# Splitting the last V load into four pieces and the wo load into twelve, in a decode kernel bound by DMA

## The chip, the cores and the metric

The kernel runs on one core of one Trainium2 chip. The metric is the device time of one execution, in microseconds (us); lower is better. The kernel before repeats within about 0.3 us on most runs, so differences of 1 us can be told, but only from several runs or from the places in the trace where they arise. "Span" is the time from the first to the last instruction in the profile; for differences under 1 us I compare spans and moments in the trace.

The profile calls the engines PE (TensorE, which multiplies matrices), DVE (VectorE), ACT (ScalarE), POOL (GpSimd) and SP (SyncE, which issues the loads; SPq in the lines below); L388 is line 388 of the kernel. It also records which share of TensorE's clock was granted: 1 ("full clock") or 0.5 ("half clock"). Lines of the profile stand here word for word; lines of a view that do not bear on the argument are left out.

## The reference, cut to what matters

Two blocks read the same two tokens (batch 2, one position, 1024 features) and are mixed by a gate: `out = g * attention(x) + (1 - g) * mlp(x)`.

```python
q = (x @ wq) as 32 heads of 128
scores = einsum(q, k_cache) * 128 ** -0.5        # k_cache: 2 x 32 x 16384 x 128, bf16
p = softmax(scores)
o = einsum(p, v_cache)                           # v_cache: the same size
a = o.reshape(2, 1, 4096) @ wo                   # wo: 4096 x 1024
...                                              # the MLP block: w1, w2, w3, w4
return g * a + (1 - g) * b
```

The two caches are 537 of the 572 MB that are read. Each byte is used once, so the kernel can hardly be faster than its loads.

## The kernel before

The caches are worked off in 32 tiles of 8 MB (two heads of one batch row). For each tile K is loaded, transposed on DVE, multiplied with q on PE (S), put through a softmax, and then V is loaded and multiplied (O). Three 8 MB buffers go round in a ring; a load is issued when its buffer is free. wo comes last, in the buffer of the last K, and takes six transfers:

```python
def load_v(i):
    t = big_tile("Vn")                             # 128 x 32768 bf16, 64 KB in a partition
    nc.sync.dma_start(out=t[:].rearrange("p (j d) -> p j d", d=Dh), in_=cache_rows(A_v_cache, i))
    vn_tiles[i] = t

WO_SPLIT = [16, 8, 4, 2, 1, 1]                     # of 32 rows; a row is 2 KB in each partition

def load_wo():
    t = big_tile("wo")[:].rearrange("p (r n) -> p r n", n=D)
    src = A_wo.rearrange("(p r) n -> p r n", p=P)
    r0 = 0
    for n in WO_SPLIT:
        nc.sync.dma_start(out=t[:, r0 : r0 + n, :], in_=src[:, r0 : r0 + n, :])
        r0 += n
```

The work that waits for these loads. Products with a piece of a tile wait only for the transfer that brings this piece.

```python
def pv_rows(V, PT, oc):                            # 64 products, in the order of j
    O = ops.tile([P, 4 * Dh], FP32, name="O")
    for m in range(NM):                            # 16
        for g in range(4):
            j0 = m * CJ + 4 * g
            nc.tensor.matmul(O[32 * g : 32 * g + 32, :], lhsT=PT[:, m : CJ * 32 : 16],
                             rhs=V[:, j0 : j0 + 4, :], start=(m == 0), stop=(m == NM - 1))
    nc.scalar.copy(out=Os[...], in_=O[:])          # then four small float32 products into oc

def wo_stage():                                    # after the last tile
    # ... Q1 = transposes of OT; q_ps = perm product; Q = copy of q_ps: needs every head
    wo = wt.pop("wo").rearrange("k r (p c) -> k r p c", c=KC)
    for r in range(32):
        for c in range(KC):                        # 8
            nc.tensor.matmul(wo_acc[:, c, :], lhsT=wo[:, r, :, c], rhs=Q[:, :, r],
                             start=(r == 0 and c == 0), stop=(r == 31 and c == KC - 1))

# the end: fin = wo_acc * g;  out_pm = fin + pre;  store out_pm (4 KB)
```

Of the kernel before, what the change touches and what calls it, by code (L numbers as in the profile page):

```python
# [23 lines left out]
def kernel(  # L24
# [15 lines left out]
    nc = tc.nc  # L40
    P = nc.NUM_PARTITIONS
    B, Sq, D = A_x.shape
    _, H, Sk, Dh = A_k_cache.shape
# [3 lines left out]
    NJ = G * Sk // P  # L47
# [8 lines left out]
    NT = B * NHG  # L56
# [16 lines left out]
    def big_tile(name):  # L73
        return big.tile([P, SLOT], BF16, tag="big", name=name)
# [7 lines left out]
    kn_tiles = {}  # L82
    vn_tiles = {}
    wt = {}

    def cache_rows(cache, i):
        b, hg = tiles[i]
        return cache[b, hg * G : (hg + 1) * G].rearrange("a s d -> (a s) d").rearrange(
            "(p j) d -> p j d", p=P
        )  # L90
# [7 lines left out]

    def load_v(i):
        t = big_tile("Vn")  # L100
        nc.sync.dma_start(
            out=t[:].rearrange("p (j d) -> p j d", d=Dh), in_=cache_rows(A_v_cache, i)
        )
        vn_tiles[i] = t

    def load_rows(keys, srcs):
# [8 lines left out]
            c0 += R * N  # L115


    WO_SPLIT = [16, 8, 4, 2, 1, 1]

    def load_wo():  # L120
        t = big_tile("wo")[:].rearrange("p (r n) -> p r n", n=D)
# [4 lines that stand above are left out]
# [7 lines left out]
    def load_first():  # L133
# [12 lines left out]
        out=perm[:].rearrange("k (h a) -> k h a", a=4),  # L146
        in_=ident_f[:].rearrange("k (a h) -> k h a", a=4),
# [24 lines left out]
    for g in range(1, 4):  # L172
        nc.vector.tensor_tensor(
            out=osel_f, in0=osel_f, in1=ident_f[:, 40 * g : 40 * g + 8], op=ALU.add
# [4 lines left out]
    for v in range(4):  # L179
        nc.gpsimd.affine_select(  # L180
            out=selv[:, v],
            in_=selv[:, v],
# [306 lines left out]
    for i in range(-1, NT):  # L489
        if i + 1 < NT:  # L490
            xfers.append(("big", f"k{i + 1}", lambda i=i: load_k(i + 1)))
            steps.append((f"k{i + 1}", lambda i=i: (build_z(i + 1), qk_stage(i + 1))))
        if i >= 0:
            xfers.append(("big", f"v{i}", lambda i=i: load_v(i)))
            steps.append((f"v{i}", lambda i=i: pv_stage(i)))
        if i + 1 < NT:
            steps.append(("", lambda i=i: softmax_stage(i + 1)))
        if i in extra:
            xfers.append(("big", f"x{i}", extra[i][0]))
            steps.append((f"x{i}", extra[i][1]))  # L500
# [19 lines left out]
    for name, run in steps:  # L520
# [9 lines left out]
        out=out_pm[:].rearrange("p b r -> p r b"), in0=fin[:], in1=pre[:], op=ALU.add  # L530
# [33 lines left out]
```

## Time and profile before

| | before |
|---|---|
| time, median of 3 runs (lowest to highest) | 1345.77 us (1345.56 to 1345.8) |
| span of the profiled run | 1344.0 us |
| DMA, mean over the span | 427 GB/s |
| last V landed whole | 1315.6 us |
| Q ready | 1324.6 us |
| first wo product, last wo product | 1325.4, 1341.0 us |
| last wo piece landed | 1335.3 us |

The page of the kernel before has the span in 40 slices; a digit is the busy share of the 16 DMA engines in tenths, and below it are the GB/s that they moved.

```profile
DMA  9999999999999999999999999999999999999995
GB/s 406 434 435 432 435 437 423 433 434 432 432 432 440 426 435 432 424 433 435 435 436 428 436 435 434 423 433 438 436 426 433 432 432 433 432 432 435 435 430 220
```

DMA is full until the last slice. A change that leaves the bytes and the instructions alone can save hardly anything outside that slice. The chain of waits that ended last, kernel before, its end (start in us, length in us, what):

```profile
1296.20 29.18 DMA wo<-in_A_wo_dram
1325.39 0.05 issue
1325.43 15.55 PE wo_acc L388 x256
1341.00 0.19 DVE fin L527
1341.21 0.23 DVE out_pm L529
```

The chain runs through the first wo piece and then through 256 wo products without a break. The timeline of the same stretch shows what came before them (start, length, engine, line, operation; in brackets how long the engine had been idle and what it waited for):

```profile
1315.68 6.23 PE L344 MATMUL O<-Vn,PT 128*32 128x512 bf16 x64 [8.89 <-DMA Vn<-in_A_v_cache_dram]
1322.60 1.05 PE L354 MATMUL misc<-osel,Os 128*128 128x2 f32 x8 [0.70 <-ACT Os L352]
1324.38 0.23 DVE L384 CAST Q<-misc 128x64 bf16<-128x64 f32 x1 [0.28 <-PE misc L382]
1325.43 15.53 PE L388 MATMUL wo_acc<-Q,wo 128*128 128x2 bf16 x256 [1.09 <-DMA wo<-in_A_wo_dram]
1341.47 0.40 SPq L533 DMA_DIRECT2D out_dram<-out_pm  x1
```

PE waits 8.9 us for the whole V, takes 6.2 us for its products, needs another 2.7 us until Q is there (1321.91 to 1324.61), waits for the first wo piece and then works off wo at 60 ns a product. The DMA issues of the end (count, KB, us from issue to landing):

```profile
wo<-in_A_wo_dram SPq DMA_DIRECT2D x1, 4096.0 KB, 29.2
wo<-in_A_wo_dram SPq DMA_DIRECT2D x1, 2048.0 KB, 33.7
wo<-in_A_wo_dram SPq DMA_DIRECT2D x2, 256.0 KB, 36.8
out_dram<-out_pm SPq DMA_DIRECT2D x1, 4.0 KB, 1.6
```

The last piece was issued at 1298.5 and landed at 1335.3. PE is busy for 5.7 us after that: products that could have run earlier, had it had work earlier.

One more view is needed. The trace has the semaphore increments of each transfer, one for each of the 16 DMA engines. They show that the engines do not finish together: the last V is done at 1304.7 us on the first engine and at 1315.6 on the last. All "landed" times in this document are those of the last engine.

### The profile page before, as it was taken

How to read it: one execution, taken by the hardware profiler on the slowest of the kernel's cores; microseconds unless marked ns; L12 is line 12 of the kernel's file. 1: busy time of each engine (PE TensorE's matmuls, PEld its weight loads, DVE VectorE, ACT ScalarE, POOL GpSimd, SP SyncE). 2: the span in 40 equal slices, each digit the busy share in tenths (PEclk: the TensorE clock that was granted, in tenths of full speed). 3: DMA queues.
4: the chain of work that ended last, by engine and by line, in shares of the span. 5: the costliest groups of instructions: out<-in, count | busy, mean ns of one | idle time of the engine just before them, and what ended most of it. 6: DMA issues, size and time to landing. Idle time of an engine off the chain costs nothing.

```text
span 1344.0 us, 12921 instructions
## 1 busy us (share of the span) xinstructions
PE 828.4 (62%) x5524; PEld 400.5 (30%) x5587; DVE 707.8 (53%) x864; ACT 45.6 (3%) x100; POOL 14.4 (1%) x45
## 2 busy tenths in 40 slices
PE   2577655576656765555676566655556765555566
PEld 2233222432225322222232423222222322222235
DVE  0666565366651665555565156565445656545560
ACT  0000000000000000000000000000000000000000
POOL 0000000000000000000000000000000000000000
PEclk9988877788776877777887588877778887777885
DMA  9999999999999999999999999999999999999995
GB/s 406 434 435 432 435 437 423 433 434 432 432 432 440 426 435 432 424 433 435 435 436 428 436 435 434 423 433 438 436 426 433 432 432 433 432 432 435 435 430 220
DMA packets 11545, 573.36 MB, mean 427 GB/s; under 512 B 1888, under 2 KB 1888, under 8 KB 2272
## 3 DMA queue, kind: packets, MB, share of 16 engines
q1 hardware_dynamic: 11488, 572.54, 98.7%
q8 instruction: 43, 0.70, 0.2%
q14 instruction: 14, 0.11, 0.0%
HBM read 572.53 MB, written 0.00 MB: 426 GB/s over the span
## 4 chain that ended last, share of the span: by engine, by line
PE 28%; DVE 23%; DMA 19%; another core or an unknown queue 13%; issue 13%; ACT 2%; SPq 0%; ACTq 0%; POOL 0%
DVE T L292 20%; DMA Kn<-in_A_k_cache_dram 17%; PE S L300 13%; PE O L344 7%; PE misc L440 3%; DMA wo<-in_A_wo_dram 2%; PE misc L354 2%; PE misc L207 2%; ACT Pr L328 1%; DVE PT L332 1%; PE wo_acc L388 1%; ACT Os L352 1%; DVE mx L321 1%; DVE mdiag L314 1%
## 5 line engine op out<-in xcount | busy, mean ns | idle before, releaser
L300 PE MATMUL S<-T,z 128*128 128x512 bf16 x1985 | 582.3, 421 | 340.9 <-DVE T L292 319.6
L292 DVE STREAM_TRANSPOSE T<-Kn 128x1024 f32<-128x1024 f32 x512 | 612.0, 1229 | 266.6 <-DMA Kn<-in_A_k_cache_dram 217.6
L300 PEld LDWEIGHTS <-z 128*128 128x128 bf16 x2048 | 218.5, 107 | 699.1 <-issue 537.1
L344 PE MATMUL O<-Vn,PT 128*32 128x512 bf16 x2048 | 120.4, 388 | 8.9 <-DMA Vn<-in_A_v_cache_dram 8.9
L371 DVE TENSOR_TENSOR OT<-misc,rinv 128x2 bf16<-128x2 f32 x32 | 5.1, 159 | 161.4 <-PE misc L354 161.4
L344 PEld LDWEIGHTS <-PT 128*32 128x32 bf16 x2048 | 73.4, 141 | 55.2 <-issue 16.8
L207 PE MATMUL misc<-rs,ones_f 128*128 128x2 f32 x64 | 17.9, 349 | 76.4 <-DVE rs L364 76.4
L352 ACT COPY Os<-O 128x512 f32<-128x512 f32 x32 | 18.8, 586 | 1091.2 <-PE O L344 1091.2
L354 PE MATMUL misc<-osel,Os 128*128 128x2 f32 x256 | 33.7, 254 | 22.2 <-ACT Os L352 22.2
L354 PEld LDWEIGHTS misc<-osel,Os 128*128 128x128 f32 x256 | 31.0, 191 | 36.7 <-ACT Os L352 36.7
L311 DVE TENSOR_REDUCE m<-S 128x1 f32<-128x512 f32 x32 | 22.2, 693 | 36.9 <-PE S L300 36.9
L440 PEld LDWEIGHTS <-wt 128*128 128x128 bf16 x576 | 35.7, 171 | 18.7 <-DMA wt<-in_B_w_dram 17.4
L207 PEld LDWEIGHTS misc<-rs,ones_f 128*128 128x128 f32 x64 | 16.1, 313 | 81.2 <-issue 78.4
L332 DVE STREAM_TRANSPOSE PT<-Pr 128x512 bf16<-128x512 bf16 x32 | 22.7, 711 | 28.7 <-ACT Pr L328 28.7
L328 ACT ACTIVATE Pr<-S,nb 128x512 bf16<-128x512 f32 x32 | 22.0, 687 | 123.6 <-DVE nb L323 120.6
L207 PE MATMUL misc<-mdiag,ones_f 128*128 128x128 f32 x64 | 15.6, 325 | 15.6 <-DVE mdiag L314 15.6
L321 DVE TENSOR_REDUCE mx<-misc 64x1 f32<-64x64 f32 x64 | 14.2, 222 | 19.0 <-PE misc L207 18.6
L270 POOL TENSOR_TENSOR z<-qsel,own 128x32 bf16<-128x32 bf16 x32 | 10.8, 337 | 1225.7 <-PE S L300 1194.5
L245 PE MATMUL misc<-xT,wt 128*128 128x2 bf16 x256 | 7.1, 165 | 25.8 <-DVE xT L240 23.1
L440 PE MATMUL misc<-xn2T,wt 128*128 128x2 bf16 x224 | 14.4, 202 | 9.1 <-DMA wt<-in_B_w_dram 9.1
L440 PE MATMUL misc<-h2T,wt 128*128 128x2 bf16 x224 | 13.6, 198 | 7.9 <-DMA wt<-in_B_w_dram 7.9
L368 DVE RECIPROCAL rinv<-misc 128x2 f32<-128x2 f32 x32 | 5.5, 171 | 22.2 <-PE misc L207 22.2
(74 smaller groups left out, 105.6 us busy)
## 6 DMA issues: line engine op xcount, KB each, us to landing
wt<-in_B_w_dram SPq DMA_DIRECT2D x2, 7168.0 KB, 50.4
wt<-in_B_w_dram SPq DMA_DIRECT2D x2, 2048.0 KB, 39.9
wo<-in_A_wo_dram SPq DMA_DIRECT2D x1, 4096.0 KB, 29.2
wo<-in_A_wo_dram SPq DMA_DIRECT2D x1, 2048.0 KB, 33.7
wo<-in_A_wo_dram SPq DMA_DIRECT2D x1, 1024.0 KB, 35.7
Kn<-in_A_k_cache_dram SPq DMA_DIRECT2D x32, 52.1
Vn<-in_A_v_cache_dram SPq DMA_DIRECT2D x32, 37.8
wo<-in_A_wo_dram SPq DMA_DIRECT2D x1, 512.0 KB, 36.5
```

Of the source, the lines that this page charges most:

```text
L207: nc.tensor.matmul(ps[:], lhsT=ones_f[:], rhs=src, start=True, stop=True)
L292: nc.vector.transpose(out=T[:].rearrange("p w j s -> p j w s"), in_=Kw[:, m * CW : (m + 1) * CW].rearrange("p (j w e) -> p j w e", w=2, e=32),
L300: nc.tensor.matmul(S[:], lhsT=z[:, v, NM - 1 - m : NM - 1 - m + P], rhs=Tb[:, v // 2, :, v % 2], start=(m == 0 and v == 0), stop=(m == NM ...
L311: nc.vector.reduce_max(out=m[:], in_=S[:], axis=AX.X)
L314: nc.vector.tensor_scalar(out=mdiag[:], in0=ident_f[:], scalar1=m[:, 0:1], scalar2=None, op0=ALU.mult)
L321: nc.vector.reduce_max(out=mx[pa, :], in_=mall[pa, pa], axis=AX.X)
L328: nc.scalar.activation(out=Pr[:], in_=S[:], func=ACTF.Exp, bias=nb[:], scale=scale, accum_out=rs[:])
L332: nc.vector.transpose(out=PT[:], in_=Pr[:])
L344: nc.tensor.matmul(O[32 * g : 32 * g + 32, :], lhsT=PT[:, m : CJ * 32 : 16], rhs=V[:, j0 : j0 + 4, :], start=(m == 0), stop=(m == NM - 1),)
L352: nc.scalar.copy(out=Os[:].rearrange("p x d -> p (x d)"), in_=O[:])
L354: nc.tensor.matmul(oc[:], lhsT=Os[:, x, :], rhs=osel[:, x, :], start=(x == 0), stop=(x == 3))
L440: nc.tensor.matmul(ps[:, c, :], lhsT=w[:, r, :].rearrange("k (p c) -> k p c", c=C)[:, :, c], rhs=actT[:, r, :], start=(r == 0), stop=(r == ...
```

## The change

It wants the products to follow the transfers closely. The V products start after half of V, not after all of it, so that only an eighth of them is left when the last byte lands; and the wo products start after 4 of 32 rows, not after 16.

```diff
+    V_SPLIT_LAST = [NJ // 2, NJ // 4, NJ // 8, NJ // 8]
@@ load_v
-        nc.sync.dma_start(
-            out=t[:].rearrange("p (j d) -> p j d", d=Dh), in_=cache_rows(A_v_cache, i)
-        )
+        tv = t[:].rearrange("p (j d) -> p j d", d=Dh)
+        src = cache_rows(A_v_cache, i)
+        j0 = 0
+        for n in V_SPLIT_LAST if i == NT - 1 else [NJ]:
+            nc.sync.dma_start(out=tv[:, j0 : j0 + n, :], in_=src[:, j0 : j0 + n, :])
+            j0 += n
@@
-    WO_SPLIT = [16, 8, 4, 2, 1, 1]
+    WO_SPLIT = [4] * 6 + [2, 2, 1, 1, 1, 1]
```

NJ is 256, the number of V rows of 128 values that each partition holds of a tile; NT is the 32 tiles.

## The prediction

> **What bounds the kernel.** DMA: the page shows the 16 engines 0.9 or more busy in 39 of 40 slices. Nothing before the last slice changes, so only the end counts. There the timeline and the transfers' semaphore increments in the trace show:
> - The last K is used up at 1296.2 us, which issues wo (six pieces) behind the last V.
> - The last V lands whole at 1315.6; its 64 products wait 8.9 us for it, start at 1315.68 and take 6.2 us.
> - Their tail (copy Os, small products, OT, transposes, permutation, Q) runs from 1321.9 to 1324.6, 2.7 us.
> - The first wo piece (16 of 32 rows) lands at 1325.4. Then 256 products run 60.7 ns apart (0.486 us a row), 15.55 us to 1340.98. The last wo piece landed at 1335.3: for the last 5.7 us PE works off a backlog. The chain of waits agrees.
>
> The 16 DMA engines finish a transfer apart (last V: 1304.7 for the first, 1315.6 for the last). A piece counts as landed when the slowest has written; the Trainium skill ("DMA: Bandwidth & Descriptors", section "Why a DMA increments its semaphore by 16 and not by 1") says the same, and this trace agrees. That engine takes 0.61 us a wo row, longer than PE's 0.486, so PE can keep up if it starts in time.
>
> **What the change does.** V in 1/2, 1/4, 1/8, 1/8 should land at about 1305.7, 1310.8, 1313.3, 1315.9. 56 of 64 products then hide under the transfer; the last eight take about 0.9 us at the half clock seen here, so Q is ready at about 1319.6 instead of 1324.6. wo in pieces of four rows lands every 2.5 us from about 1318.4, so PE starts at 1319.6 instead of 1325.4, catches up by the third or fourth piece and then waits for each. The end is the last landing plus one row's products.
>
> **What it adds.** Smaller packets: by median record 2 KB takes 84 ns, 4 KB 160, 8 KB 312, 16 KB 613, 32 KB 1215, 64 KB 2420. On the slow engine (8 packets per transfer) that is about 0.3 us for V, 0.5 for wo, and some 0.03 for each of nine more transfers: last landing about 1336.1 instead of 1335.3. Nine more issues on SP (0.33 to 0.43 us) are hidden. The trace shows eight transfer semaphores used in turn; 16 transfers at the end reuse them, so later wo issues may wait for earlier pieces. I cost that at nothing: the slow engine would still have several pieces queued.
>
> **Sum.** PE ends at 1336.1 + 0.1 + 0.49 = 1336.7 instead of 1341.0: 4.3 us saved of about 1346. Either half alone gains little: V alone is held by the first wo piece at 1325.4, wo alone by Q at 1324.6 (under 1 us).
>
> **Predicted:** 1341.4 us, range 1340.2 to 1343.2. Faster by over 2%: 0.01; within 2%: 0.98; slower: 0.01.
>
> **Right if** the after-profile shows: V products in four bursts, the last of about eight; Q by 1319.6; wo products starting near 1319 with many short waits on wo transfers; last wo landing 1335.5 to 1336.8, PE ending under 1 us later.
>
> **Wrong if** products wait for the whole V or wo tile (gain near 0); reuse of semaphores holds an issue until an engine runs dry (last landing over 1 us later, gain 1 to 3); small packets cost more than their record says; or the spread between DMA engines comes out otherwise.

## The result, and the profile after

| | before | after |
|---|---|---|
| time, median (lowest to highest), 4 runs each | 1345.78 us (1345.56 to 1345.82) | 1342.47 us (1342.14 to 1343.39) |
| span of the profiled run | 1344.0 us | 1340.6 us |
| Q ready | 1324.61 us | 1320.46 us |
| last wo piece landed | 1335.31 us | 1335.87 us |
| last wo product done | 1340.98 us | 1336.71 us |
| output store, issue to landing | 1.58 us | 2.52 us |

The ratio is 0.9977, with a 95% interval of 0.996 to 0.9994. It is the mean time of the one kernel's runs over that of the other's of the same rounds, so not quite the ratio of the medians. The change saves 3.3 us, a quarter of a per cent: outside the noise.

The chain of waits, kernel after, its end:

```profile
1263.36 46.54 DMA Vn<-in_A_v_cache_dram
1309.92 20.80 DMA wo<-in_A_wo_dram
1330.72 0.05 issue
1330.77 5.95 PE wo_acc L392 x96
1336.74 0.19 DVE fin L531
1336.95 0.23 DVE out_pm L533
```

Only 96 of the 256 wo products are left on the chain after its last wait for a transfer. The timeline of the kernel after:

```profile
1307.14 5.35 PE L348 MATMUL O<-Vn,PT 128*32 128x512 bf16 x48
1313.36 0.66 PE L348 MATMUL O<-Vn,PT 128*32 128x512 bf16 x8 [0.87 <-DMA Vn<-in_A_v_cache_dram]
1315.85 1.08 PE L348 MATMUL O<-Vn,PT 128*32 128x512 bf16 x8 [1.83 <-DMA Vn<-in_A_v_cache_dram]
1317.62 1.87 PE L358 MATMUL misc<-osel,Os 128*128 128x2 f32 x8 [0.69 <-ACT Os L356]
1320.23 0.23 DVE L388 CAST Q<-misc 128x64 bf16<-128x64 f32 x1 [0.30 <-PE misc L386]
1320.51 9.86 PE L392 MATMUL wo_acc<-Q,wo 128*128 128x2 bf16 x160 [0.32 <-DVE Q L388]
1330.77 5.93 PE L392 MATMUL wo_acc<-Q,wo 128*128 128x2 bf16 x96 [0.39 <-DMA wo<-in_A_wo_dram]
1337.20 0.40 SPq L537 DMA_DIRECT2D out_dram<-out_pm  x1
```

V works as intended: 56 of 64 products lie under the transfer (in three bursts and not four, since PE was still at work on the first piece when the second landed at 1309.9). wo starts 4.9 us earlier. But PE does not "wait for each piece": in the wo stage it waits 0.39 us once in this view and is busy otherwise. That wait is for the sixth wo piece, the last one of four rows, which lands at 1330.72 us; the 96 products behind it then run through. The DMA issues of the end, kernel after:

```profile
wo<-in_A_wo_dram SPq DMA_DIRECT2D x6, 1024.0 KB, 23.5
wo<-in_A_wo_dram SPq DMA_DIRECT2D x4, 256.0 KB, 12.8
out_dram<-out_pm SPq DMA_DIRECT2D x1, 4.0 KB, 2.5
```

The late pieces land 12.8 us after their issue and not 36.8, because they are issued late. The trace shows eight transfer semaphores used in turn. With four V and twelve wo transfers, the ninth to the sixteenth of the last loads each had to wait until an earlier one of them had landed; the last was issued at 1325.8 and not at 1298.5. Seven of the 16 engines ran dry before each of the last two pieces (their increments for the last one come at 1327.9 to 1328.2 us, over 2 us after its issue). That did no harm to the landings: the slowest engine still had pieces queued. Then the output store: 2.5 us where it had been 1.6. This was not in my sum.

### The profile page after: what moved, and what is told of

It reads as the page before. It is cut to its first block, busy times and chain, and to the rows that moved or that the text cites. A ratio compares the mean times of both kernels' runs of the same rounds, so it can differ in the third digit from the quotient of the medians.

```text
span 1340.6 us, 12993 instructions
## 1 busy us (share of the span) xinstructions
PE 845.7 (63%) x5587; PEld 402.6 (30%) x5587; DVE 707.6 (53%) x864; ACT 45.5 (3%) x100; POOL 14.4 (1%) x45
## 4 chain that ended last, share of the span: by engine, by line
PE 27%; DVE 22%; DMA 22%; another core or an unknown queue 13%; issue 13%; ACT 2%; SPq 0%; ACTq 0%; POOL 0%
DVE T L296 19%; DMA Kn<-in_A_k_cache_dram 17%; PE S L304 13%; PE O L348 7%; DMA Vn<-in_A_v_cache_dram 3%; PE misc L444 3%; PE misc L358 2%; PE misc L211 2%; DMA wo<-in_A_wo_dram 2%; ACT Pr L332 1%; DVE PT L336 1%; ACT Os L356 1%; DVE mx L325 1%; DVE mdiag L318 1%
## 5 line engine op out<-in xcount | busy, mean ns | idle before, releaser
L304 PE MATMUL S<-T,z 128*128 128x512 bf16 x2048 | 597.6, 425 | 326.1 <-DVE T L296 310.6
## 6 DMA issues: line engine op xcount, KB each, us to landing
wo<-in_A_wo_dram SPq DMA_DIRECT2D x4, 256.0 KB, 12.8
```

The lines of the kernel that those rows point to most:

```text
L304: nc.tensor.matmul(S[:], lhsT=z[:, v, NM - 1 - m : NM - 1 - m + P], rhs=Tb[:, v // 2, :, v % 2], start=(m == 0 and v == 0), stop=(m == NM ...
```

## The experiments

All of the results below matched the reference within the comparison's tolerance, k7r4 and contig included; for contig this means only that the tolerance does not see its permuted wo columns. "Time" is the median with that of the kernel before on the same chip.

### Is one half of the change enough? v_only and wo_only

v_only keeps the new V and takes back wo; wo_only the other way round.

```diff
# v_only, against the kernel after            # wo_only, against the kernel before
-WO_SPLIT = [4] * 6 + [2, 2, 1, 1, 1, 1]      -WO_SPLIT = [16, 8, 4, 2, 1, 1]
+WO_SPLIT = [16, 8, 4, 2, 1, 1]               +WO_SPLIT = [4] * 6 + [2, 2, 1, 1, 1, 1]
```

> V in four pieces, wo in its six old ones. Theory A (the two halves need each other: Q comes early, but the first wo piece of 16 rows still lands at about 1325.7): Q ready at 1320.5 as in the changed kernel, wo products start at 1325.7 and run 15.5 us without a wait to 1341.2, time within 0.5 us of the kernel before (1345.8). Rival B (the V split is what pays, wo only follows): most of the 3.3 us gain is here, 1342.5 to 1343.5.

> wo in twelve pieces, V whole. Theory A: three wo pieces have landed when Q is ready at 1324.6, the 256 products run from 1324.7 without a wait to 1340.2, so 0.8 us earlier than before: 1344.5 to 1345.3. Rival C (the fine wo pieces are what pays): 1342.5 to 1343.5.

Measured: v_only 1346.03 us against 1345.63 (5 runs, span 1344.3); wo_only 1344.32 against 1345.63 (5 runs, 1344.13 to 1345.58). The ratios to the kernel before are 1.0003 (0.999 to 1.0015) and 0.9992 (0.998 to 1.0005), so both intervals include no change; that of after_again, below, does not (0.9979, 0.9965 to 0.9992). The timeline of v_only, its last products:

```profile
1315.88 1.08 PE L348 MATMUL O<-Vn,PT 128*32 128x512 bf16 x8 [1.83 <-DMA Vn<-in_A_v_cache_dram]
1325.64 15.54 PE L392 MATMUL wo_acc<-Q,wo 128*128 128x2 bf16 x256 [5.42 <-DMA wo<-in_A_wo_dram]
```

Q comes early and then PE sits idle 5.4 us for the first wo piece: the V split alone gains nothing. The timeline of wo_only:

```profile
1315.44 5.22 PE L344 MATMUL O<-Vn,PT 128*32 128x512 bf16 x64 [8.54 <-DMA Vn<-in_A_v_cache_dram]
1323.42 15.48 PE L388 MATMUL wo_acc<-Q,wo 128*128 128x2 bf16 x256 [0.32 <-DVE Q L384]
```

Here wo waits for Q only, and the 256 products run through. Gains of -0.4 and 1.3 us alone, and 2.7 us together on the same chip (after_again below): each half uncovers the wait that the other takes away. Rivals B and C, that one half pays, fall.

The 1.3 us are more than my 0.8. One cause is visible: the 64 V products took 5.22 us, not 6.23. The clock records of the trace have the full clock granted from about 1318.7 us here, and from 1320.9 in the kernel before. The Trainium skill ("TensorE: Matmul & The Clock Gate", Part 1) says that the clock is decided in a free-running window of 3413 ns; the clock records of these traces agree, with full-clock stretches of 3413 and 6827 ns. The runs of wo_only fall into two groups of spans, 1342.1 to 1342.5 and 1343.3 to 1343.8, some 1 us apart. I take them for early and late windows, but only the profiled run has a trace, so that is not shown.

### The change again, and a delayed store: after_again and after_delay

```diff
# after_delay, against the kernel after
     nc.vector.tensor_tensor(out=fin[:], in0=wo_acc[:], in1=over_r(g_bc[:]), op=ALU.mult)
+    for _ in range(24):
+        nc.vector.tensor_scalar(out=fin[:], in0=fin[:], scalar1=1.0, scalar2=None, op0=ALU.mult)
```

> The changed kernel itself, on the chip of the other runs: 1342.1 to 1343.4, output store again about 2.5 us from issue to landing, against 1.6 in the kernel before; if that was chance, 1.6 here.

> The changed kernel with 24 dependent multiplications by one (0.21 us each, 5.0 us together) on DVE before the output store. Theory S (the store takes 2.5 instead of 1.6 us because it comes 1.3 us after the last wo landing and not 6 us after it): issue to landing back at about 1.6 us, so the span grows by 4.1 us only. Rival (the store is slower for another reason, such as the semaphore or the number of transfers before it): 2.5 us again, the span grows by 5.0.

Measured: after_again 1342.93 us against 1345.63 (5 runs, 1342.01 to 1343.36; spans 1340.2 to 1341.0), store 2.8 us. after_delay 1347.57 us, span 1345.5, store:

```profile
DMA to landing us min/median/max: 2.4/2.4/2.4
```

So the slow store is no chance, and its closeness to the last loads is not the cause: theory S falls. The span grew by 4.9 us in the profiled run: the 5.0 that were added, less some 0.1 us each for an earlier last landing and a store of 2.4 instead of 2.5 us.

### What holds the end now? contig

```diff
-        wo = wt.pop("wo").rearrange("k r (p c) -> k r p c", c=KC)
+        wo = wt.pop("wo").rearrange("k r (c p) -> k r p c", c=KC)      # wrong columns, on purpose
```

> Wrong result on purpose: the changed kernel, but each wo product takes 128 neighbouring columns as weights instead of every eighth. All 256 wo products ran exactly 60 ns apart so far, at half clock and at full clock alike, while the wq products (neighbouring columns) ran 25.5 ns apart. Theory D (the stride sets the 60 ns, and after the change PE and the wo transfer end almost together): pace 25 to 40 ns, PE now waits for every piece as the prediction had it, and yet ends at about 1336.3, only 0.3 to 0.5 us earlier, because the last piece still lands at 1335.9. Rival (PE's backlog is what holds the end): PE ends 2 us or more earlier.

Measured: 1342.45 us against 1345.96 (4 runs, 1341.91 to 1343.06; spans 1340.1 to 1340.4). The timeline of contig, wo products, five of ten lines:

```profile
1320.39 1.84 PE L392 MATMUL wo_acc<-Q,wo 128*128 128x2 bf16 x64 [0.32 <-DVE Q L388]
1323.20 1.02 PE L392 MATMUL wo_acc<-Q,wo 128*128 128x2 bf16 x32 [0.96 <-DMA wo<-in_A_wo_dram]
1325.69 1.02 PE L392 MATMUL wo_acc<-Q,wo 128*128 128x2 bf16 x32 [1.48 <-DMA wo<-in_A_wo_dram]
...
1335.17 0.38 PE L392 MATMUL wo_acc<-Q,wo 128*128 128x2 bf16 x8 [0.28 <-DMA wo<-in_A_wo_dram]
1335.80 0.37 PE L392 MATMUL wo_acc<-Q,wo 128*128 128x2 bf16 x8 [0.26 <-DMA wo<-in_A_wo_dram]
```

With PE twice as fast (64 products in 1.84 us, 29 ns each, instead of 60), the picture is the one that I had predicted for the change: many short waits, one for each piece. And yet PE ends at 1336.19, only 0.52 us before the kernel after, because the last piece still lands at 1335.76. So after the change two bounds lie within half a microsecond of each other: PE (15.5 us of products from 1320.5 us on) and the wo transfer. A gain on one side alone is cut off by the other.

By the way: the 60 ns are the stride. In wo_only, whose first wo products ran at full clock, and in the kernel before at half clock, they are exactly 60.0 ns apart; with neighbouring columns it is 29 to 32 ns at half clock, and 25.5 ns for the wq products at full clock.

### Sparing the late DMA engine: k7r4

The last landing is late because one engine lags 11 us behind the first. wo rows 16 to 19 were cut by partitions, to give them to few engines that might be idle.

```diff
-        for n in WO_SPLIT:
-            nc.sync.dma_start(out=t[:, r0 : r0 + n, :], in_=src[:, r0 : r0 + n, :])
+        for n, cut in WO_SPLIT:             # cut = 119 for rows 16 to 19, else 0
+            for p0, p1 in ((0, cut), (cut, P)):
+                if p1 > p0:
+                    nc.sync.dma_start(out=t[p0:p1, r0 : r0 + n, :], in_=src[p0:p1, r0 : r0 + n, :])
```

> The changed kernel with wo rows 16 to 19 cut at partition 119: one transfer of 119 partitions, one of 9. By the Trainium skill (DMA: Bandwidth & Descriptors, Why a DMA increments its semaphore by 16 and not by 1) a transfer runs on the largest number of engines up to 16 that divides its slowest dimension, the lowest numbered: 7 and 9 here. Theory E (the last landing is late only because one DMA engine lags 11 us behind the first seven): if those seven are the lowest numbered, the late engine is spared four rows (2.4 us), the last wo piece lands at about 1333.4, and PE, now alone in the way with 15.5 us of products from 1320.5, ends at 1336.0: time 0.5 to 0.7 us below the changed kernel. If the lowest numbered are the late ones, they get 5.3 us of packets instead of 2.4 and the last landing moves to about 1338.8.

Measured: 1352.76 us against 1345.96, 10 us worse than the change. The timeline, two of its waits:

```profile
1326.31 2.10 PE L396 MATMUL wo_acc<-Q,wo 128*128 128x2 bf16 x32 [3.13 <-DMA wo<-in_A_wo_dram]
1339.66 2.07 PE L396 MATMUL wo_acc<-Q,wo 128*128 128x2 bf16 x32 [4.20 <-DMA wo<-in_A_wo_dram]
```

The semaphores of the two cut transfers climb by 7 and by 9 late increments, so the engine counts are those that the skill gives. But the 119 partitions landed at 1339.2 us, and the last wo piece at 1347.2 instead of the 1338.8 of the bad case. The experiment did more than it was meant to: pieces that were queued ahead of the 119 partitions landed up to 7.6 us late too (the fourth at 1333.32 us, in the kernel after at 1325.74), and the 8 KB packets took 590 ns in the median between 1317 and 1323 us, where they take 312 otherwise. Which engines are the late ones is not settled by it: of the seven, four were done at 1325 to 1326 us and three only after 1335, so they are not all of one kind. It shows that this way of sharing out the load costs more than it spares.

### Why does one engine lag? dve_more

```diff
             T = t_tile([P, 2, CJ, 32], FP32)
+            nc.vector.memset(spare[:], 0.0)          # 128 x 1, read by nobody; 512 of them
             nc.vector.transpose(
```

> The changed kernel with 512 more DVE instructions that nobody waits for (a memset of one column before each K transpose; DVE is idle 47% of the time). The lag of the slowest DMA engine grew in steps of 0.96 us, about every 120 us, together with the 8 KB transfers of the runtime's queue 14, and DVE has 1351 instructions. Theory G (those are fetches of DVE's instructions, 128 in each, and they run on the slowest engine, ahead of or between its packets): four more fetches, lag 10.8 + 3.8 = 14.6 us, last wo landing and time 3.8 us later, 1346 to 1347. Rival (the lag has another cause): time within 0.5 us of the changed kernel, lag 10.8.

Measured: 1347.81 us against 1345.96 (4 runs), 4.9 us more than the median of after_again (another chip), span 1345.4; the last wo piece landed at 1340.24 instead of 1335.87. That is near what theory G forecast, but this run does not show theory G, because it did not run as its source is written. In the trace all 512 memsets are over by 121.5 us, in bunches; what moved them there is not on record. The timeline of dve_more:

```profile
99.53 9.59 DVE L297 MEMSET spare<- 128x1 f32 x77
113.72 7.70 DVE L297 MEMSET spare<- 128x1 f32 x62
121.47 1.24 DVE L298 STREAM_TRANSPOSE T<-Kn 128x1024 f32<-128x1024 f32 x1
142.03 0.33 SPq L106 DMA_DIRECT2D Vn<-in_A_v_cache_dram  x1
```

The same two steps in the timeline of the kernel after:

```profile
101.88 2.35 DVE L296 STREAM_TRANSPOSE T<-Kn 128x1024 f32<-128x1024 f32 x2
122.48 0.33 SPq L106 DMA_DIRECT2D Vn<-in_A_v_cache_dram  x1
```

The third K tile had landed by 104.06 us, but DVE was busy with memsets and began on it at 121.47 (kernel after: landed at 101.70, begun at 101.88). So its buffer came free 19.5 us later, and the next V load was issued at 142.03 us and not at 122.48. The first engine had finished its last load at 138.66 us by then and the last one did at 143.76, so the engines ran dry: this V landed on the first engine at 163.34 us instead of 158.04, on the last at 165.04 instead of 159.93. That is a delay of over 5 us in the whole stream, without any fetch; 4.4 us of it are left at the last landing. That the time fell close to the forecast is luck.

What the trace does show of the fetches comes before that. The 8 KB transfers of queue 14 went from 14 to 18, four more as expected; the packets of 16 KB stayed at 43 or 44, about one for 256 of PE's instructions. By 124 us there had been five 8 KB transfers (at 10, 26, 48, 98 and 118 us), where the kernel after had had one, and the slowest engine was 5.07 us behind the first, where in the kernel after it was 1.88 us behind; the other fifteen engines lay within 1.72 us as before. DVE had run 622 instructions by then against 142, which fits one fetch for about 128 of them. So four fetches more go with 3.2 us more lag on one engine. When the engines ran dry this lag was lost (1.70 us at 165 us), which is why the lag at the end was 9.85 us and not 14.6. The kernel after has the same pattern: the lag of its slowest engine rises by 0.9 to 1.0 us between the landings around each of the fetches at 683, 941, 1063, 1192 and 1311 us. That such a fetch costs time at the end is tested by best, below, and not by this run.

### Fewer pieces: fewer and fewer_again

```diff
-    V_SPLIT_LAST = [NJ // 2, NJ // 4, NJ // 8, NJ // 8]
+    V_SPLIT_LAST = [3 * NJ // 4, NJ // 8, NJ // 8]
-    WO_SPLIT = [4] * 6 + [2, 2, 1, 1, 1, 1]
+    WO_SPLIT = [5, 6, 5, 4, 4, 3, 2, 2, 1]
```

> V in 3/4, 1/8, 1/8 and wo in nine pieces (5, 6, 5, 4, 4, 3, 2, 2, 1 rows): 12 transfers at the end instead of 16. Theory F (the slow output store of the changed kernel, 2.4 to 2.8 us from issue to landing against 1.6, goes with the number of transfers or with the late issues before it): about 1.6 to 2.0 here. PE ends at 1336.4 to 1336.8 as in the changed kernel, since PE products up to the last V piece now run without a pause and Q comes up to 1 us earlier; time 1341.3 to 1342.0. If the store stays at 2.5 us: 1342.3 to 1342.9.

> The parent of the last run, on the same chip: 1341.7 to 1342.3, about 1 us faster than the change as given; store issue to landing again 1.6 us.

Measured: 1341.95 us against 1345.96 (ratio 0.997) and, on the chip of after_again, 1341.53 against 1345.65 (ratio 0.9969; 0.2 us below the expected range), so about 1 us better than the change as given (on the chip of after_again 1.4 us in the median time, 0.8 us in the median span). The timeline of fewer:

```profile
1309.98 5.11 PE L348 MATMUL O<-Vn,PT 128*32 128x512 bf16 x56 [2.28 <-DMA Vn<-in_A_v_cache_dram]
1315.86 0.66 PE L348 MATMUL O<-Vn,PT 128*32 128x512 bf16 x8 [0.77 <-DMA Vn<-in_A_v_cache_dram]
1319.26 2.52 PE L392 MATMUL wo_acc<-Q,wo 128*128 128x2 bf16 x40 [0.32 <-DVE Q L388]
```

With three quarters of V in the first piece PE has no long pause before the last one; its last eight products take 0.66 us, not 1.08, and Q comes at 1319.2, 1.3 us earlier. (That the shorter pause is the reason is not shown: after_delay and no_small, with a pause of 1.83 us, took 0.66 us too. When full clock was granted differs from run to run.) The early Q is not what paid: PE still ended its products at 1336.75 us, since wo landed no earlier. What paid is the store, back at 1.6 us in both runs.

### What makes the store slow? no_small and late_few

```diff
# no_small, against the kernel after           # late_few, against the kernel before
-WO_SPLIT = [4] * 6 + [2, 2, 1, 1, 1, 1]       -WO_SPLIT = [16, 8, 4, 2, 1, 1]
+WO_SPLIT = [3] * 8 + [2] * 4                  +WO_SPLIT = [10, 6, 4, 3, 2, 2, 2, 1, 1, 1]
```

> The changed kernel with wo in eight pieces of three rows and four of two: again 16 transfers at the end, the last four issued late, but no packet of 2 KB (512 of them in the change as given, 128 in the run with 12 transfers, 256 in the kernel before). Theory H (the number of transfers, or the late issues that it forces, makes the output store slow): store 2.4 to 2.8 us. Rival (the 2 KB packets do): 1.6 us. PE ends at about 1337, later than in the change as given because the last piece has two rows.

> V whole, wo in ten pieces (10, 6, 4, 3, 2, 2, 2, 1, 1, 1 rows): 11 transfers at the end, fewer than the 12 with which the output store was fast, but the last one can be issued only when the second wo piece has landed at about 1325.5, when the fast DMA engines have run dry (in the kernel before they finish wo at about 1324.4). Theory late (issues that come after engines have run dry go with the slow store): issue to landing 2.0 us or more. Theory count (the number of transfers does): 1.6 us. Time as in the run with wo alone split, 1344.1 to 1345.6.

Measured: no_small 1343.06 us against 1345.65, store 2.7 us: small packets are not the cause. late_few 1345.03 us against 1345.65, and its last wo piece was indeed issued late, at 1325.4, to engines that had run dry (they finished it 8 us apart, and the piece before it 10.8), but its store:

```profile
DMA to landing us min/median/max: 1.6/1.6/1.6
```

| transfers of the last V and wo | runs | store, issue to landing |
|---|---|---|
| 7 to 12 | before, v_only (10), late_few (11), fewer, fewer_again and best (12) | 1.6 us |
| 13 | wo_only | 2.0 us |
| 16 | after, after_again, after_delay, contig, dve_more, no_small | 2.4 to 2.9 us |
| 17 | k7r4 | about 3.0 us (by its increments) |

Small packets and closeness to the loads are ruled out as the cause, and so is a single piece that reaches engines which have run dry (late_few); the number of transfers fits all fourteen runs. Two rivals are not separated from it. With eight semaphores, the number of transfers beyond eight is also the number of issues that were held back. And in every run with a slow store two pieces or more reached dry engines, in late_few only one. So it stays a correlation, with one store traced in each run: in the kernel after, the packets of the store begin as soon after its issue as in the kernel before (0.9 us), but with 16 transfers some of the 16 increments come 1.0 to 1.5 us after the first, where with 7 to 12 they all come within 0.2 us. What the number of transfers does to them is open.

### A version that beats both: best

fewer, with two small DVE operations of every tile moved to engines that are idle.

```diff
-        nc.vector.tensor_scalar(out=mdiag[:], in0=ident_f[:], scalar1=m[:, 0:1], scalar2=None, op0=ALU.mult)
+        nc.scalar.mul(out=mdiag[:], in_=ident_f[:], mul=m[:, 0:1])
-        nc.vector.tensor_scalar(out=rs2[:], in0=hmask[:], scalar1=rs[:, 0:1], scalar2=None, op0=ALU.mult)
+        nc.gpsimd.tensor_scalar(out=rs2[:], in0=hmask[:], scalar1=rs[:, 0:1], scalar2=None, op0=ALU.mult)
```

> The run with 12 transfers at the end (V in 3/4, 1/8, 1/8; wo in 5, 6, 5, 4, 4, 3, 2, 2, 1) with two small DVE operations of every tile moved away: mdiag to ACT, rs2 to GpSimd, so some 64 to 96 of DVE's 1351 instructions go. Theory G (each 128 DVE instructions cost one fetch of 8 KB, which holds the slowest DMA engine about 1 us): one fetch fewer, everything at the end about 1 us earlier, last wo landing 1334.7 instead of 1335.7, time 1340.7 to 1341.2. Rival (fetches cost nothing there): same time as its parent, within 0.2 us, or slower by the changed softmax chain.

Measured: 1340.52 us against 1345.65 (5 runs; ratio 0.9964, 0.995 to 0.9978), and its parent 1341.53 on the same chip. The chain of waits, best, its end:

```profile
1297.16 32.26 DMA wo<-in_A_wo_dram
1329.42 0.04 issue
1329.47 6.06 PE wo_acc L390 x96
1335.56 0.19 DVE fin L529
```

The last wo piece landed at 1334.49 us, 1.18 us earlier than in its parent, and everything after it moved along. DVE has 1256 instructions instead of 1351. The 8 KB fetches still number 14, because ACT has more instructions now, but those at DVE's pace are ten instead of eleven. In the parent an 8 KB fetch falls at 1311 us, and the lag of the slowest engine goes from 10.04 to 10.97 us between the first and the second V piece; in best the last such fetch comes at 1284 us and the lag stays at 9.92 and 9.94. The first engine landed the last V piece at 1304.72 us in best and at 1304.79 in its parent, so the rest of the stream did not move. This run, and not dve_more, is what theory G rests on: one DVE fetch fewer, and the slowest engine lands about 1 us earlier. The time and the last landing lie 0.2 us below the expected 1340.7 and 1334.7.

## Why the prediction was right or wrong

The time, 1342.47 us, lies in the range of 1340.2 to 1343.2, and 1.1 us above the 1341.4 that were named. Point by point:

- **What bounds the end: right.** Before the change, PE worked off a backlog for 5.7 us after the last landing; v_only and wo_only show that both waits had to go. V alone gained nothing and wo alone 1.3 us ("under 1 us" was said; in its profiled run an earlier switch to the full clock shortened the V products by 1.0 us).
- **V pieces: right to within 0.9 us.** They landed at 1305.0, 1309.9, 1313.3 and 1315.8 us; 1305.7, 1310.8, 1313.3 and 1315.9 were predicted.
- **Cost of small packets and of semaphores used again: right.** The last wo piece landed at 1335.87 us (1336.1 predicted). Late issues held up no landing of the slowest engine.
- **"Q is ready at about 1319.6": mis-sized by 0.9 us.** Q came at 1320.46. I had taken the 2.7 us of the tail from the kernel before, where the clock had reached full speed when it ran. The clock records show the full clock from 1320.9 to 1324.3 us there, which covers the tail's eight small products; in the kernel after from 1312.4 to 1315.8, which ends as the last V piece lands. PE ran the tail at half clock: its eight small products took 1.87 us, not 1.05. (In fewer the full clock lasts from 1313.8 to 1320.7, and Q comes at 1319.2.)
- **"Catches up by the third or fourth piece and then waits for each": wrong.** PE caught up at the sixth piece, the last one of four rows (landed at 1330.72 us), and not again: it needs 5.9 us for the 12 rows left, and the transfers bring them within 5.15 us. The late Q cost nothing here. PE ended 6.0 to 6.1 us after the last four-row piece had landed in after, after_delay, fewer and best alike, with Q at 1320.5, 1319.9, 1319.2 and 1318.4 us. Only contig, with products at 29 to 32 ns, showed the predicted waits. The end of PE, 1336.71 us, came out at the predicted 1336.7 by luck: the last landing was 0.2 us earlier than predicted, and PE ended 0.84 us after it instead of 0.6.
- **The sum: one term was missing.** "4.3 us saved" is what PE saved (1340.98 to 1336.71, 4.27 us). After that the output store took 2.52 instead of 1.58 us, and 0.94 us of the gain went there. In the span 3.4 us were left, in the median of the time 3.3. I had carried over the store from the kernel before without naming it as a term. It is nearly all of the 1.1 us by which the time missed the forecast; the range was wide enough to hold it, but nothing in the forecast foresaw it. The experiments show that it goes with the number of transfers; with 12 instead of 16 of them the term vanishes. Why is open.

## What to carry to other kernels

When the last loads are split so that work can follow them, split all of the loads that the end waits for: a wait that is removed uncovers the next one, and the second often makes the first worth nothing. Count the pieces as well: enough that the consumer never runs dry and that the last piece is small, and no more; here 12 transfers did the work of 16 and were 1 us faster. In a kernel bound by its loads, instructions on an engine that is half idle are not free, because fetching them takes DMA time (best: one fetch fewer, 1.2 us earlier at the last landing); look at which DMA engine lands last and what else it carries. And look in the trace whether an experiment ran as it is written: dve_more met its forecast for another reason.

## What the Trainium skill lacked or had wrong

- "Runtime: NRT & Kernel Launch", section "Instruction fetch mechanics", calls the cost of crossing a block boundary mostly hidden. Here it is not: 95 DVE instructions fewer (with 64 more on ACT and 32 more on GpSimd) saved one of DVE's fetches, and the last landing came 1.2 us earlier; in dve_more four fetches more by 124 us went with 3.2 us more lag of one DMA engine. DVE's appear here as blocks of 8 KB; the page gives 16 KB for each engine's refills, which agrees with the 16 KB packets of the profile's instruction queue.
- "DMA: Bandwidth & Descriptors", section "Why a DMA increments its semaphore by 16 and not by 1", says that the engines of a transfer finish independently. It has no figure for how far apart: 0.5 us at the start of this kernel, 11.0 us at its end, in steps that go with instruction fetches.
- The same page has nothing on a small store being slower after many transfers: 4 KB took 1.6 us from issue to landing after 7 to 12 transfers of the last loads, 2.0 after 13, and 2.4 to 3.0 after 16 or 17.
- The same section gives the rule for how many engines a transfer uses. It doesn't say that a transfer over few engines can slow the others' packets: 8 KB packets went from 312 to about 590 ns beside one of 119 partitions.
- "TensorE: Matmul & The Clock Gate", section "Weight-path perf modes", lists packed and strided weights for its fast loading alike. Here every eighth bf16 column cost 60.0 ns a product at half clock and at full clock, neighbouring columns 29 to 32 ns at half clock and 25.5 at full clock.
